# Order of the last steps of a weight fold, and the unread products ahead of it, in a fused attention and feed-forward kernel

## The chip, the cores and the metric

The kernel runs on one core of a Trainium2 chip. The metric is the device time of one execution in microseconds (us); lower is better. A core has TensorE (PE, matrix products; PEld is its loading of weights), VectorE (DVE), ScalarE (ACT), GpSimd (POOL) and SyncE (SP), which here issues nearly all DMA transfers. The engines run side by side, each in its own program order, and wait for each other by semaphores.

## The reference

```python
kv = einsum('bhsd,bhse->bhde', k, v)           # 8 batches, 8 heads, 576 x 64
out = einsum('bhsd,bhde->bhse', q, kv)
rms = sqrt(mean(out * out, axis=-1) + 1e-06)
x = (out / rms * g_norm), heads side by side   # 4608 x 512
a, b = x @ w1, x @ w2                          # 512 x 1024 each
h = (a * b) @ w3                               # 1024 x 1024
return h @ w_out                               # 1024 x 512
```

The weights come as 64-bit floats and are used as 32-bit floats.

## The kernel before, in words

`w3 @ w_out` doesn't depend on the tokens, so the kernel first folds the two into one matrix of 1024 x 512 (`w3o_sb`). That is the fold, the first 81 us. Then it goes over nine groups of 512 tokens: per group, attention, the gates (`x @ w1`, `x @ w2` and their product) and the projection by the folded matrix, the last two with a Winograd scheme that saves products by sums. The attention of the first batch is worked out between the fold's products.

**Conversion of weights.** A 64-bit weight tile (`raw`, four buffers, loaded at L207) is turned into 32-bit floats by two ScalarE passes (L165 for the low words, L167 for the high words) and four VectorE passes (L169, L173, L176, L181), with a scaling by g (L135) for w1 and w2. `begin_next` issues ScalarE's two, `end_next` the others and the next load; a conversion is a generator, so single steps can be issued apart.

**The fold.** `w3` is used in two halves of its columns, each in eight chunks of 128 rows. For each chunk TensorE transposes the piece of `w3` by four transposes (`turn_w3`, L701), ScalarE copies the result out of PSUM (L703) and `fold_chunk` runs four products of 512 columns (L717; in the first chunk eight of 256). A 32-bit product is two records in the trace. In the second half, chunks 3, 5 and 7 are transposed by a DMA instead: the words are taken apart (L308), the DMA transposes (L310), and a ScalarE copy, here called the join, puts the words together (L320, `ab<-chunks`). For chunk 7, "the eighth", the join was placed in iteration c = 5.

**Unread products.** `keep_warm(n, small)` (L282 to L287) issues n products of the identity with itself at 128 x 128, and `small` ones at 16 x 16. Nobody reads them. They stand at the start, before and after the first `turn_w3`, and once more (two) after the first chunk's fold.

**Attention of the first batch in the fold.** In iterations c = 1 and c = 4 `begin_q` transposes q and `begin_kv` works out kv; in c = 2 and c = 5 `product` computes the attention product (L425) and its norm: ScalarE squares two banks (L392), VectorE sums each (L393), ScalarE takes the root (L397), VectorE inverts it (L399) and multiplies (L402, two halves `xn`). The norm is a generator with a pause after the sums and one after the root. The first product's `xn` is taken apart by ScalarE (L306), transposed by two DMAs, and put together by VectorE (`x_by_dma`, L320, `xT<-xn`, "x's copies"). The second product's `xn` is transposed by TensorE at c = 7 (`turn`, L461) and copied by ScalarE (L463). Three fold products come after it, and then the gates of the first group (L748).

**What sets the order.** In this part the order on TensorE, VectorE, ScalarE, GpSimd and SyncE is that of the program (a manual schedule), so moving a call in the loop over c moves its instructions in the queues of its engines. Iteration c = 5 is the one that matters here: ahead of the fold's products it issues x's copies and then, for the weight tile whose conversion is under way, the three passes L169, L173 and L176 (one `next` on the conversion).

Of the kernel before, what the change touches and what calls it, by code (L numbers as in the profile page):

```python
# [22 lines left out]
def kernel(  # L23
# [60 lines left out]
    def bank(pool, tag):  # L84
        return pool.tile([P, 512], FP32, name=tag, tag=tag)
# [6 lines left out]
    def load_q(b, r):  # L92
        t = loaded["q", b, r] = inp.tile([P, 2, J * D], FP32, name="q_sb")
        nc.sync.dma_start(
            out=t, in_=q[b, 2 * r:2 * r + 2, 0:G, :].rearrange("h (p j) d -> p h (j d)", j=J)
        )

    def load_four(names, b, g):

        for name in names:  # L100
            t = loaded[name, b, g] = inp.tile([P, 2, JS * D], FP32, name=f"{name}_sb", bufs=1)
            src = dict(k=k, v=v)[name][b, 4 * g:4 * g + 4]
            src = src.rearrange("(r e) (p j) d -> (e p) r (j d)", e=2, j=JS)
            nc.sync.dma_start(out=t, in_=src)
# [95 lines left out]
    def load_next():  # L200
        if len(raws) == len(todo):
            return
        what, i = todo[len(raws)]
        raw = raw_tile()

        def load(where, src):
            nc.sync.dma_start(out=raw[:, where].rearrange("p (c m) -> p c m", c=src.shape[1]), in_=src)  # L207

        if what == "w":
            for n, w in enumerate((w1, w2)):  # L210
                src = w[:, i * P:(i + 1) * P].rearrange("(c p) f -> p c f", p=P)
                load(slice(n * 512, (n + 1) * 512), src)
        elif what == "b":
            for h in range(2):
                src = w3[DF // 2:DF, (2 * i + h) * P:(2 * i + h + 1) * P]
                load(slice(h * 512, (h + 1) * 512), src.rearrange("(m p) f -> p m f", p=P))
        else:
            src = w3[0:DF // 2, i * P:(i + 1) * P].rearrange("(m p) f -> p m f", p=P)
            cols = w_out[i * P:(i + 1) * P, :].rearrange("p (c f) -> p c f", c=1)

            n = 1 if i else 2
            for h in range(n):
                load(slice(h * 512 // n, (h + 1) * 512 // n), src[:, h * NH // n:(h + 1) * NH // n, :])
            for h in range(n):
                f = slice(h * DM // n, (h + 1) * DM // n)
                load(slice(512 + f.start, 512 + f.stop), cols[:, :, f])
        raws.append(raw)
# [21 lines left out]
    def begin_next(between=None, at=1):  # L249

        if len(begun) < len(todo):
            begun.append(conversions(len(begun)))
            for n, (c, _) in enumerate((c, i) for c in begun[-1] for i in range(2)):
                if between is not None and n == at:
                    between()
                next(c)

    def end_next(load=True):
        for c in begun[len(converted)]:
            all_of(c)  # L260
        converted.append(len(converted))
        if load:
            load_next()

    def all_of(steps):
        for _ in steps:
            pass
# [14 lines left out]
    def keep_warm(n, small=0):  # L282

        t = bank(ps_mm, "mm")
        for i in range(n + small):
            w = P if i < n else 16
            nc.tensor.matmul(t[0:w, 0:w], lhsT=ident[:, 0:w], rhs=ident[:, 0:w], start=True, stop=True)  # L287
# [409 lines left out]
    def turn_w3(half, c):  # L697
        t_ps = bank(ps_at, "at").rearrange("p (m f) -> p m f", m=NH)
        for m in range(NH):
            src = chunks[:, c, 0, m * P:(m + 1) * P]  # L700
            nc.tensor.transpose(t_ps[:, m, :], src, ident)  # L701

        nc.scalar.copy(place_w3(half, c), t_ps)  # L703
# [711 lines left out]
    with tc.manual_schedule(  # L1415
        engines={mybir.EngineType.DVE, mybir.EngineType.Activation, mybir.EngineType.SP}
    ):
        for _ in range(RAW):
            load_next()
        nc.scalar.activation(const.tile([P, 1], FP32, name="warm"), eps_col, AF.Sqrt)  # L1420
        g_row = const.tile([1, P], FP32, name="g_row")
        for e in range(2):
            nc.scalar.dma_start(
                out=g_row[:, e * D:(e + 1) * D], in_=g_norm.rearrange("(o d) -> o d", o=1)
            )


        keep_warm(14, 11)
        begin_next()
        end_next()  # L1430
        turn_w3(0, 0)
        keep_warm(6)
        begin_next()

        g_ps = bank(ps_at, "at")[:, 0:1]
        nc.tensor.transpose(g_ps, g_row, ident[0:1, 0:1])
        nc.scalar.copy(g_col, g_ps)
        for c in range(KF):

            if c > 2:  # L1440
                begin_next()
            end_next()
            if c == 4:
                load_four("k", 0, 0)
                load_q(0, 0)
            elif c == 5:
                load_four("v", 0, 0)
                load_q(0, 1)
                load_q_left(0)
            if c == 0:  # L1450
                for n in range(2):
                    fold_chunk(0, c, range(NH), slice(n * N, (n + 1) * N))
                begin_next(lambda: turn_w3(0, 1))
                keep_warm(2)
                continue
            fold_chunk(0, c, range(NH - 1))
            if c < 3:
                begin_next(lambda: turn_w3(0, c + 1), 2)
            else:
                turn_w3(*((0, c + 1) if c + 1 < KF else (1, 0)))  # L1460
            fold_chunk(0, c, [NH - 1])


        first = batch(0)
        first.start()
        BEGIN, PRODUCT = {1: 0, 4: 1}, {2: 0, 5: 1}
        norms = {}
        FIRST = len(converted) + KF - 1
        turns, SPLIT = {}, {0: 3, 2: 5, 4: 7}
        for c in range(KF):  # L1470
            if c in BEGIN:
                first.begin_q(2 * BEGIN[c], 2 * BEGIN[c] + 1)
                if c == max(BEGIN):
                    x_first = first.x_by_dma(0, nc.vector.tensor_copy, split=nc.scalar.copy)
                    next(x_first)
                    next(x_first)
                    all_of(turns[c + 1])
            if c - 1 in norms:
                all_of(norms[c - 1])
            if c < KF - 2:  # L1480
                if c < max(BEGIN):
                    begin_next()
                if c == max(BEGIN) + 1:
                    all_of(x_first)
                    for steps_of_w in begun[len(converted)]:
                        next(steps_of_w)
                else:
                    end_next(False)
                if c in SPLIT:
                    t = turns[SPLIT[c]] = w3_by_dma(SPLIT[c])  # L1490
                    next(t)
                    next(t)
                if len(raws) < FIRST:
                    load_next()
                if c == 2:
                    for steps_of_w in begun[len(converted)]:
                        next(steps_of_w)
                elif c == max(BEGIN):
                    run(sum_w(0))
            elif c == KF - 2:  # L1500
                end_next(False)
            fold_chunk(1, c, [0])
            if c in BEGIN:
                first.begin_kv(BEGIN[c])
                if c == max(BEGIN):
                    load_q_left(1)
            if c + 1 == KF:
                for r in range(2):
                    first.turn(2 + r)
                run(combine_x(0))  # L1510
                end_next(False)
                for _ in range(3):
                    load_next()
            fold_chunk(1, c, range(1, NH - 1))
            if c == 2:
                all_of(turns[c + 1])
            elif c + 1 < KF and c + 1 not in turns:
                turn_w3(1, c + 1)
                if c + 2 in turns and c > max(BEGIN):
                    all_of(turns[c + 2])  # L1520
            if c in (max(BEGIN), KF - 2):
                begin_next()
            fold_chunk(1, c, [NH - 1])
            if c in PRODUCT:
                norms[c] = first.product(PRODUCT[c])
                next(norms[c])
                next(norms[c])
    fold_cm.__exit__(None, None, None)
    late_pool = ctx.enter_context(tc.tile_pool(name="late", bufs=1, reuse_waits="tile"))
# [179 lines left out]
```

## Time and profile before

| | us |
|---|---|
| median of three runs (lowest, highest) | 741.62 (741.22, 742.58) |
| the profiled execution's own time | 742.19 |
| its span, first to last instruction | 740.4 |
| TensorE busy | 735.3 |
| VectorE busy | 628.1 |
| ScalarE busy | 378.7 |
| DMA, HBM traffic over the span | 204 GB/s |

The profile is one execution, and its times are counted from the start of the span. A line of the timeline has the start, the duration, the engine, the line of the program, the operation, the tile written and the tile read, and how often; in brackets stands the idle time ahead of it and what ended it. Lines that follow each other on one engine may be merged. In the lines of a groups or waits view the numbers are the total, how often, and the longest. Matmuls overlap in the array and their ends are modelled, so a busy TensorE isn't TensorE at its peak.

### The profile page before, as it was taken

The page shows a single profiled execution, that of the slowest core. Times are in us where ns is not written, and L with a number is a line of the kernel's source. Part 1 is how long each engine was busy: PE and PEld are TensorE (multiplying, and loading weights), DVE is VectorE, ACT ScalarE, POOL GpSimd, SP SyncE. Part 2 cuts the span into 40 slices and gives each one's busy share as a digit, 9 for nine tenths or more (in the row PEclk, how much of TensorE's full clock was granted, in tenths as well). Part 3 has the DMA queues.
Part 4 walks back from the last instruction along what each step waited for, and adds up shares of the span by engine and source line. Part 5 has one row for each costly group of instructions (what it writes and reads, how often), then busy time and mean ns, then how long its engine had stood idle before and what let it go on. Part 6 is the DMA issues. An engine that isn't in the chain of part 4 may idle for free.

```text
span 740.4 us, 16916 instructions
## 1 busy us (share of the span) xinstructions
PE 735.3 (99%) x6863; PEld 660.5 (89%) x6863; DVE 628.1 (85%) x1259; ACT 378.7 (51%) x660; POOL 22.2 (3%) x29
## 2 busy tenths in 40 slices
PE   9999999999999999999999999999999999999998
PEld 7455788888899999999999999999999999999998
DVE  6987898968869689968996899689969987997797
ACT  6787777415552675257526752576177313212321
POOL 0000000132000000000000001000001000000000
PEclk9999999999999999999999999999999999999999
DMA  9999934599989698859986998598847762465354
GB/s 314 331 342 240 288 108 134 131 347 297 318 262 320 174 278 261 268 162 291 260 263 174 281 258 265 179 284 237 275 101 221 222 212 87 175 216 165 130 198 143
DMA packets 138769, 170.44 MB, mean 230 GB/s; under 512 B 81220, under 2 KB 114116, under 8 KB 138692
## 3 DMA queue, kind: packets, MB, share of 16 engines
q1 hardware_dynamic: 136240, 155.02, 70.6%
q10 hardware_dynamic: 2452, 14.35, 5.7%
q8 instruction: 54, 0.88, 0.5%
q14 instruction: 23, 0.19, 0.1%
HBM read 130.55 MB, written 20.71 MB: 204 GB/s over the span
## 4 chain that ended last, share of the span: by engine, by line
PE 97%; ACT 1%; DVE 1%; DMA 1%; issue 0%; POOL 0%; SPq 0%; DVEq 0%; POOLq 0%
PE mm L748 38%; PE mm L1298 23%; PE mm L1040 21%; PE mm L717 6%; PE at L347 2%; PE at L748 2%; PE mm L287 1%; PE mm L425 1%; PE at L425 1%; PE at L701 1%; DMA xn<-xT 1%; PE at L1341 0%; PE at L444 0%; DVE inv L393 0%; ACT xT L306 0%
## 5 line engine op out<-in xcount | busy, mean ns | idle before, releaser
L1089 ACT COPY slots<-mm 128x512 f32<-128x512 f32 x88 | 51.6, 586 | 127.0 <-PE mm L1298 83.7
L748 PE MATMUL mm<-xT,w_sb 128*128 128x256 f32 x448 | 102.9, 379 | 0.0
L748 PEld LDWEIGHTS mm<-xT,w_sb 128*128 128x128 f32 x448 | 84.4, 190 | 11.5 <-issue 0.5
L748 PE MATMUL mm<-xc,ws 128*128 128x256 f32 x336 | 76.1, 379 | 0.0
L748 PEld LDWEIGHTS mm<-xc,ws 128*128 128x128 f32 x336 | 63.9, 190 | 8.7
L766 ACT COPY slots<-mm 128x512 f32<-128x512 f32 x59 | 34.5, 585 | 70.6 <-PE mm L748 65.6
L717 PE MATMUL mm<-chunks,ab 128*128 128x512 f32 (+1 forms) x136 | 59.9, 578 | 0.3 <-ACT ab L703 0.2
L1093 DVE TENSOR_TENSOR slots<-mm,slots 128x512 f32<-128x512 f32 x66 | 45.1, 683 | 17.2 <-PE mm L1040 17.1
L1090 ACT COPY slots<-mm 128x384 f32<-128x384 f32 x88 | 42.3, 481 | 26.3 <-PE mm L1298 23.8
L1040 PE MATMUL mm<-ws,w3o_sb 128*128 128x128 f32 x350 | 53.9, 275 | 0.0
L1298 PE MATMUL mm<-w3o_sb,ab 128*128 128x128 f32 x368 | 48.9, 276 | 0.0
L393 DVE TENSOR_REDUCE inv<-sq 128x8 f32<-128x512 f32 (+1 forms) x40 | 24.6, 630 | 27.2 <-ACT sq L392 27.2
L1040 PEld LDWEIGHTS mm<-ws,w3o_sb 128*128 128x128 f32 x350 | 46.4, 192 | 0.0
L1298 PEld LDWEIGHTS mm<-w3o_sb,ab 128*128 128x128 f32 x368 | 45.4, 192 | 0.6
L717 PEld LDWEIGHTS mm<-chunks,ab 128*128 128x128 f32 x136 | 23.6, 190 | 22.5 <-issue 15.5
L1298 PE MATMUL mm<-w3o_sb,raw 128*128 128x128 f32 x340 | 43.5, 275 | 0.0
L1298 PEld LDWEIGHTS mm<-w3o_sb,raw 128*128 128x128 f32 x340 | 40.7, 192 | 0.0
L748 PE MATMUL mm<-xc,w_sb 128*128 128x256 f32 x160 | 38.5, 384 | 0.0
L1094 DVE TENSOR_TENSOR slots<-mm,slots 128x384 f32<-128x384 f32 x66 | 36.3, 551 | 2.2 <-PE mm L1298 1.6
L748 PE MATMUL mm<-xT,ws 128*128 128x256 f32 x160 | 38.1, 381 | 0.0
L748 PEld LDWEIGHTS mm<-xT,ws 128*128 128x128 f32 x160 | 30.1, 190 | 4.3 <-ACT slots L766 0.2
L748 PEld LDWEIGHTS mm<-xc,w_sb 128*128 128x128 f32 x160 | 29.8, 190 | 4.2
(246 smaller groups left out, 1650.0 us busy)
## 6 DMA issues: line engine op xcount, KB each, us to landing
w3o_sb<-w_l SPq DMA_DIRECT2D x21, 896.0 KB, 5.6
w3o_sb<-w3o_l SPq DMA_DIRECT2D x18, 896.0 KB, 6.0
raw<-in_moe_w_dram SPq DMA_DIRECT2D x31, 512.0 KB, 7.5
raw<-w3o_l SPq DMA_DIRECT2D x15, 896.0 KB, 4.7
w3o_sb<-w3o_l ACTq DMA_DIRECT2D x14, 896.0 KB, 4.6
k_sb<-in_k_dram SPq DMA_DIRECT2D x16, 576.0 KB, 5.7
v_sb<-in_v_dram SPq DMA_DIRECT2D x16, 576.0 KB, 6.3
q_sb<-in_q_dram SPq DMA_DIRECT2D x32, 256.0 KB, 4.8
```

The costliest lines, as they stand in the source:

```text
L347: nc.tensor.matmul(ps[r * D:(r + 1) * D, :], lhsT=k_sb[rows, r, cols], rhs=v_sb[rows, r, cols], start=(j == 0), stop=(j == JS - 1),)
L393: adds["norm"] = nc.vector.tensor_reduce(out=inv[:, i], in_=sq.rearrange("p (h d) -> p h d", d=D), axis=AX.X, op=ALU.add)
L425: nc.tensor.matmul(o_ps[l][tokens, n * D:(n + 1) * D], lhsT=qT[r][rows, e, i, tokens], rhs=kv_b[rows, m // 2 ^ l, e, h, :], start=True, st ...
L717: nc.tensor.matmul(sums_ps[half][m][:, cols], lhsT=w3T[half, c][:, m, :], rhs=chunks[:, c, 1, cols], start=(c == 0 and cols.start == 0), s ...
L748: nc.tensor.matmul(ps[:, u, :], lhsT=lhsT(a_name, u, c), rhs=rhs(b_name, c),  start=(u == 0 and c == 0 and new), stop=(c == chunks - 1), s ...
L766: copies.setdefault(name, []).append(nc.scalar.copy(t, ps))
L1040: nc.tensor.matmul(ps[place // 4][:, place % 4, :], lhsT=x, rhs=y, start=new and place // 4 not in seen, stop=True, skip_group_check=True,)
L1089: nc.scalar.copy(z[:, 0:4], ps[0])
L1090: return nc.scalar.copy(z[:, 4:7], ps[1][:, 0:3])
L1093: nc.vector.tensor_add(z[:, 0:4], ps[0], z[:, 0:4])
L1094: nc.vector.tensor_add(z[:, 4:7], ps[1][:, 0:3], z[:, 4:7])
L1298: nc.tensor.matmul(ps[place // 4][:, place % 4, :], lhsT=x[:, c, :], rhs=y[:, c, :], start=new and place // 4 not in seen, stop=(c == 1), ...
```

## The change

Three things are done, and the numbers of instructions of each kind stay as they are but for the unread products.

1. At the start, ahead of the first transposes, 11 large unread products instead of 14 large and 11 small. Behind these transposes, 1 large and 21 small instead of 6 large.
2. In iteration c = 5 the three VectorE passes over a weight tile (L169, L173, L176) are issued ahead of x's copies (L320) and not behind them.
3. In the same iteration the join of the eighth chunk (ScalarE, L320 `ab<-chunks`) is issued behind the two squares of the second norm and ahead of its root, not ahead of the squares.

The orders of SyncE and GpSimd, and so of the DMA transfers, are the same in both kernels.

```diff
-        keep_warm(14, 11)
+        keep_warm(11)
         begin_next()
         end_next()
         turn_w3(0, 0)
-        keep_warm(6)
+        keep_warm(1, 21)
         begin_next()
...
                 if c == max(BEGIN) + 1:
-                    all_of(x_first)
                     for steps_of_w in begun[len(converted)]:
                         next(steps_of_w)
+                    all_of(x_first)
                 else:
                     end_next(False)
...
             elif c + 1 < KF and c + 1 not in turns:
                 turn_w3(1, c + 1)
-                if c + 2 in turns and c > max(BEGIN):
-                    all_of(turns[c + 2])
             if c in (max(BEGIN), KF - 2):
                 begin_next()
             fold_chunk(1, c, [NH - 1])
             if c in PRODUCT:
                 norms[c] = first.product(PRODUCT[c])
                 next(norms[c])
+                if c > max(BEGIN):
+                    all_of(turns[c + 2])
                 next(norms[c])
```

## The prediction

> **What bounds the kernel now.** I read the page first: busy shares, then the chain that ended last.
>
> ```profile
> span 740.4 us, 16916 instructions
> PE 735.3 (99%) x6863; PEld 660.5 (89%) x6863; DVE 628.1 (85%) x1259; ACT 378.7 (51%) x660; POOL 22.2 (3%) x29
> PE 97%; ACT 1%; DVE 1%; DMA 1%; issue 0%; POOL 0%; SPq 0%; DVEq 0%; POOLq 0%
> ```
>
> TensorE bounds the kernel: it has work in 735.3 of 740.4 us. Next, what it waited for in the whole run:
>
> ```profile
> PE mm L287 <- POOL ident masks.py:199: 1.4, 1, 1.4
> PE at L461 <- DVE xn L402: 0.5, 2, 0.3
> PE mm L717 <- ACT ab L703: 0.2, 1, 0.2
> ```
>
> From about 79 us to the last transposes nothing is listed: TensorE is never seen to wait there. So the change can win only ahead of 79 us, in two places: the unread products (L287), which count as busy but give nothing, and the two waits at L461. Whatever is won there comes through, if no other engine then falls behind. The timeline of the start:
>
> ```profile
> 6.50 0.43 DVE L181 CUSTOM_DVE_ANT_0 chunks<-chunks,ab 128x512 uint16<-128x512 uint16 x1
> 7.38 0.42 ACT L167 ACTIVATE chunks<-raw 128x256 f32<-128x256 f32 x1
> 7.89 0.66 PE L701 MATMUL at<-ident,chunks 128*128 128x128 f32 x4
> 8.38 1.50 PE L287 MATMUL mm<-ident 128*128 128x128 f32 x12
> 8.58 0.58 ACT L703 COPY ab<-at 128x512 f32<-128x512 f32 x1 [0.77 <-PE at L701]
> 9.81 0.22 PE L1436 MATMUL at<-ident,g_row 1*128 1x1 f32 x1
> ```
>
> The data of the first transposes are there at 6.93 (6.50 + 0.43), but TensorE, still in unread products, starts them at 7.89. The copy of their result is done at 9.16; the fold's first product starts at 9.96, behind six more unread products. So the unread products, not the data, set the start. The timeline of the end of the fold:
>
> ```profile
> 71.43 1.30 DVE L320 COPY xT<-xn 128x1024 uint16<-128x1024 uint16 x2 [2.47 <-ACT ab L703]
> 72.33 1.17 ACT L320 COPY ab<-chunks 128x1024 uint16<-128x1024 uint16 x1 [1.00 <-DMA chunks<-ab]
> 72.65 0.75 DVE L169 TENSOR_SCALAR ab<-raw 128x1024 uint16<-128x1024 uint16 x1
> 73.28 0.68 DVE L173 TENSOR_SCALAR w_sb<-w_sb 128x1024 f32<-128x1024 f32 x1
> 73.40 1.07 ACT L392 ACTIVATE sq<-at 128x512 f32<-128x512 f32 x2
> 74.00 0.69 DVE L176 TENSOR_SCALAR w_sb<-w_sb 128x1024 uint32<-128x1024 uint32 x1
> 74.61 1.27 DVE L393 TENSOR_REDUCE inv<-sq 128x8 f32<-128x512 f32 x2
> 75.91 0.31 ACT L397 ACTIVATE inv<-inv,eps_col 128x16 f32<-128x16 f32 x1 [1.44 <-DVE inv L393]
> 76.61 1.29 DVE L402 TENSOR_TENSOR xn<-at,inv 128x512 f32<-128x512 f32 x2
> 77.35 0.33 PE L461 MATMUL at<-ident,xn 128*128 128x128 f32 x1 [0.20 <-DVE xn L402]
> 77.95 0.98 PE L461 MATMUL at<-ident,xn 128*128 128x128 f32 x7 [0.27 <-DVE xn L402]
> ```
>
> VectorE sits idle for 2.47 us (68.97 to 71.43), then its three weight passes stand ahead of the reduces; ScalarE puts the join ahead of the squares, though the attention product was done at 72.66. TensorE pays at L461.
>
> **Part 1: the unread products.** A 128-wide unread product is two records. In the profile 22 records fill the first 4.85 us (windows view, 1.35 to 6.20), 0.213 us each; later (8.38) they come every 0.111. So TensorE ran at half rate for the first 5.4 us. The page's clock row (tenths of 40 slices) is too coarse to show it.
>
> Removed at first: 3 large (6 records) and 11 small. The 11 that stay end at 6.20. Two transposes follow at once (their quarter was ready at 5.44), the third waits until 6.98, the fourth's result is there by 7.36. ScalarE is in L167 until 7.80, so the copy L703 runs 7.80 to 8.38 instead of 8.58 to 9.16. Meanwhile TensorE does one large product (0.22) and 21 small ones: 42 records. In the profile 22 small records took 0.61 us (windows view, 7.24 to 7.85), nearly 0.025 us apart, so 42 take 1.05. From 7.20: 0.22, 0.1 for the change of shape, 1.05, then 0.1 and 0.15 around the transpose of g (L1436, as in the trace): the fold's first product at 8.82, not 9.96: **−1.14 us**. It is the small products, not the copy (8.38), that set it.
>
> Does the rest follow? The fold of chunk 0 ends at 12.38; chunk 1's first half is ready at 11.95 even as before. Its second half was ready at 13.81 and will be wanted at 13.65; but VectorE had idled 0.46 behind ScalarE's L165 at 9.06, which can now start when its load lands (2.80 + 5.8 = 8.6), so 13.4. If that cover fails, 0.16 is lost. For chunk 2 VectorE had waited 1.16 at 15.34 for a pass queued behind L703: that goes with TensorE. From there VectorE needs 3.75 us a chunk and TensorE 3.96. Loads: chunk 6 lands at 24.5 and is read at 26.7, 2.2 us of cover.
>
> What no row shows is the pace of small products at half rate. Below: 0.025, as seen. Above: twice that, as the large ones do (0.213 to 0.111), 1.05 us more, and the part is worth 0.1. I take 0.025, since in the profile the clock had doubled at 6.8, before they start.
>
> A rule speaks against the change here. The trace doubled its rate 5.4 us after the first product. The Trainium skill ("TensorE: Matmul & The Clock Gate", Part 1: The HAM clock gate) says that the clock is released after one busy window of about 3.4 us, free-running, so the moment differs between runs; its Part 4 says that transposes don't count as busy in the same way. By that rule, windows that end after 6.2 are less busy than before, and some executions would be released a window (3.4 us) later: the estimate from the page is about 1 us back in these runs. No row here shows it.
>
> **Part 2: weight passes first.** Nothing is added; L169, L173, L176 (0.75, 0.68, 0.69) go into the idle 2.47 us. L169's input ends at 68.73, L173's at 69.76 (ScalarE, 68.63 + 1.13), so they run 68.97 to 71.2, and the x copies, whose transposes land at 71.3, keep their 71.43. Cost nothing, cover 0.2 us; if gone, the reduces still have 0.6. No DMA is in the moved steps, and SP's and POOL's orders are unchanged. One load that waited 0.5 us for L176 may start earlier: 0 to a trifle.
>
> **Part 3: the join behind the squares.** Squares at 72.72 (0.06 behind the product, as in the first norm, 57.66 to 57.72) instead of 73.40, to 73.79. Reduces at 73.36 and 73.96 (copies done 72.73) to 74.63. The join, whose data land at 72.3, now runs 73.70 to 74.87; root at about 74.8 (ScalarE's starts lie 1.07 apart behind such a copy), not 75.91: 1.1 us earlier. The root is thus held by the join for some 0.1 us, no more. Normalized halves at 76.2 and 76.8, not 77.3 and 77.9. TensorE's last product starts at 76.55, so it wants them at 76.98 and 77.1: both waits go. Without them eight transposes take 0.87 (0.109 each) and the next product starts at 77.86 instead of 78.77: **−0.91 us**; the view's 0.47 understates it, since the ends of products are modelled and count as busy beyond the next possible start. Queued behind the later join are the root, the next weight passes (L165, L167), L723 and the x copies L463: all still earlier than before by about 0.8. TensorE wants the join's result for the eighth chunk at 75.7 (weight load); it is there at 74.9. What is late next: the second normalized half, 0.3 us of cover.
>
> **Sum:** 742.19 (profiled: span 740.4 and 1.79 around it) − 1.14 − 0.91 = **740.1**. The median of the runs shown is 741.62, so −0.2% of it. The runs spread from 741.22 to 742.58; a release of the clock earlier or later than 6.8 moves the old start of the fold (1 us earlier release, six to nine records from half to full rate, 0.5 us), while the new one, which waits for data at 6.98, hardly moves. I therefore sum from the profile and not from the median.
>
> **Rivals.** *Half the gain:* one of the two is lost to something not seen, say the first 14 us catch up with the conversions (13.81), or another engine is late further on, since TensorE arrives 2 us earlier everywhere and covers there can't be read from a view without waits. 742.19 − 1.14 = 741.05 or 742.19 − 0.91 = 741.28. For: VectorE is 92% busy from 10 to 41 us (28.48 of 31.0). Against: its waits there are for ScalarE, which waits for TensorE.
>
> *Slower: the clock is released late.* With only transposes, gaps and 16-wide products between 6.2 and 8.8, the work there may not count. If TensorE then needs as much full work again as at the start (5.4 us) from the fold's first product on, half of it, 2.7, is lost, and up to 1.05 more in the small products: 743.0 to 744.0 (740.14 + 2.7 to + 3.75). It decides where half rate lasts beyond about 4 us into the fold. For: the trace holds no case of so little work before a release. Against: large products still fill 1.35 to 6.20, and 22 small records and four transposes (7.24 to 8.38) did not take the rate back.
>
> **Chances.** Forecast 0.62, from 739.7 (fold bound by the copy, 0.4 earlier) to 740.8; half the gain 0.23, 740.8 to 741.5; late clock 0.15. "Within 0.2%" (about what a measurement of this kernel can tell from no change) begins at 740.14, on the forecast itself: of its 0.62 I put 0.47 beyond, since the four times shown average 741.9, over the median, and 0.15 within. Faster 0.47, same 0.15 + 0.23 = 0.38, slower 0.15. The range is 739.7 to 741.5, which leaves the late clock out.
>
> **What would show it.** The fold's first L717 at 8.8; no wait at L461 and its eight transposes in one row; L169 at 69 minus 1.1, ahead of L320; squares, join, root in this order, root about 1.1 us after the squares end. Wrong: unread or fold products 0.43 us apart in the 256-wide records after 9 us (late clock), a wait of L717 at 13.6 for L181, or new waits of TensorE after 79 us.

## The result, and the profile after

| | before | after |
|---|---|---|
| median, us (16 runs each) | 742.38 | 740.40 |
| lowest and highest | 741.22, 743.29 | 740.02, 740.94 |
| profiled execution, own time | 742.19 | 740.67 |
| its span | 740.4 | 738.8 |

The change makes the kernel 1.98 us faster by the medians; the ratio is 0.9975, with a 95% interval of 0.9968 to 0.9983. The median of before over 16 runs lies 0.76 above that of the three runs shown ahead of the prediction. Between the two profiled executions the difference is 1.52, less than between the medians. The runs after lie closer together: within 0.92 us, before within 2.07.

The page after still has TensorE as the bound. But the chain now has a transfer in it, 2% `raw` and SyncE, where before it had 1% `xn`:

```profile
span 738.8 us, 16924 instructions
PE 733.8 (99%) x6867; PEld 659.5 (89%) x6867; DVE 629.1 (85%) x1259; ACT 378.9 (51%) x660; POOL 22.2 (3%) x29
PE 94%; DMA 2%; ACT 2%; DVE 1%; SPq 1%; issue 0%; ACTq 0%
```

What TensorE waited for in the whole run after:

```profile
PE mm L287 <- POOL ident masks.py:199: 1.4, 1, 1.4
PE mm L717 <- DVE chunks L181: 0.5, 1, 0.5
PE mm L748 <- ACT inner_sums L766: 0.3, 1, 0.3
```

The waits at L461 are gone. Two others are there in their place: one in the fold's second chunk, at L181 where there had been 0.2 at L703, and one in the gates, at L748, where before had none. The timeline of the start, after:

```profile
1.35 5.06 PE L287 MATMUL mm<-ident 128*128 128x128 f32 x22 [1.35 <-POOL ident masks.py:199]
6.21 1.02 PE L701 MATMUL at<-ident,chunks 128*128 128x128 f32 x4
6.30 0.42 DVE L181 CUSTOM_DVE_ANT_0 chunks<-chunks,ab 128x512 uint16<-128x512 uint16 x1
8.10 0.57 ACT L703 COPY ab<-at 128x512 f32<-128x512 f32 x1
8.53 0.22 PE L1436 MATMUL at<-ident,g_row 1*128 1x1 f32 x1
8.72 3.72 PE L717 MATMUL mm<-chunks,ab 128*128 128x256 f32 x16
```

The transposes now stand around the end of the second quarter's conversion (6.72), and the fold starts at 8.72 instead of 9.96, 0.05 behind the end of the copy (8.67). The timeline of the end of the fold, after:

```profile
67.71 0.75 DVE L169 TENSOR_SCALAR ab<-raw 128x1024 uint16<-128x1024 uint16 x1
69.37 0.69 DVE L176 TENSOR_SCALAR w_sb<-w_sb 128x1024 uint32<-128x1024 uint32 x1
70.31 1.30 DVE L320 COPY xT<-xn 128x1024 uint16<-128x1024 uint16 x2 [0.25 <-DMA xn<-xT]
71.58 1.09 ACT L392 ACTIVATE sq<-at 128x512 f32<-128x512 f32 x2 [1.44 <-PE at L425]
72.21 1.28 DVE L393 TENSOR_REDUCE inv<-sq 128x8 f32<-128x512 f32 x2 [0.60 <-ACT sq L392]
72.55 1.16 ACT L320 COPY ab<-chunks 128x1024 uint16<-128x1024 uint16 x1
73.60 0.32 ACT L397 ACTIVATE inv<-inv,eps_col 128x16 f32<-128x16 f32 x1
74.31 1.29 DVE L402 TENSOR_TENSOR xn<-at,inv 128x512 f32<-128x512 f32 x2
75.80 1.04 PE L461 MATMUL at<-ident,xn 128*128 128x128 f32 x8
```

The passes fill VectorE's idle time, the sums start with the first square's end, the join stands between squares and root, and the eight transposes of L461 are one row. The new wait stands four microseconds behind the fold's last product, at the third product of the gates:

```profile
79.25 1.89 PE L748 MATMUL mm<-xT,w_sb 128*128 128x256 f32 x8
80.97 1.89 PE L748 MATMUL mm<-xc,ws 128*128 128x256 f32 x8
83.12 1.13 PE L748 MATMUL mm<-xc,ws 128*128 128x256 f32 x4 [0.26 <-ACT inner_sums L766]
```

The chain of waits after, followed back from there, says what it hangs on (start, duration, what):

```profile
71.60 0.62 SPq L207
...
72.27 8.51 DMA raw<-in_moe_w_dram
...
80.94 0.25 ACT ab L165
...
82.01 0.57 ACT w3o_sb L723
82.58 0.49 ACT inner_sums L766
83.08 0.04 issue
83.12 2.00 PE mm L748 x8
```

A load of `raw` lands at 80.78; ScalarE's L165 waits for it, and queued behind L165 are L723 and L766, whose bank the third product wants. The timeline after names another for this wait, VectorE's L169, which ends at 80.79:

```profile
80.04 0.75 DVE L169 TENSOR_SCALAR ab<-raw 128x1024 uint16<-128x1024 uint16 x1
80.94 1.17 ACT L165 ACTIVATE ab<-raw 128x1024 f32<-128x1024 uint32 x1 [1.46 <-DVE ab L169]
```

The same two before:

```profile
81.48 1.20 ACT L165 ACTIVATE ab<-raw 128x1024 f32<-128x1024 uint32 x1
82.33 0.75 DVE L169 TENSOR_SCALAR ab<-raw 128x1024 uint16<-128x1024 uint16 x1
```

There L165 started without a wait and 0.85 ahead of this L169, so it doesn't need it, and the load is what is left.

How far TensorE is ahead of before, product by product: 1.24 at the fold's first product, 0.95 at chunk 1 (13.84 for 14.79), 1.17 from chunk 2 (17.79 for 18.96), 1.19 ahead of L461, 2.10 behind it (76.67 for 78.77) and at the first product of the gates (79.25 for 81.35), 1.57 from the second record of the third on (83.44 for 85.02), 1.54 at the end.

### The profile page after: what moved, and what is told of

Its sections match the earlier page's. It is cut to its first block, busy times and chain, and to the rows that moved or that the text cites. A ratio compares the mean times of both kernels' runs of the same rounds, so it can differ in the third digit from the quotient of the medians.

```text
span 738.8 us, 16924 instructions
## 1 busy us (share of the span) xinstructions
PE 733.8 (99%) x6867; PEld 659.5 (89%) x6867; DVE 629.1 (85%) x1259; ACT 378.9 (51%) x660; POOL 22.2 (3%) x29
## 4 chain that ended last, share of the span: by engine, by line
PE 94%; DMA 2%; ACT 2%; DVE 1%; SPq 1%; issue 0%; ACTq 0%
PE mm L748 37%; PE mm L1298 23%; PE mm L1040 21%; PE mm L717 5%; PE at L347 2%; DMA raw<-in_moe_w_dram 2%; PE at L748 2%; PE mm L425 1%; PE at L425 1%; PE at L701 1%; PE at L1341 0%; ACT ab L165 0%; SPq L207 0%; PE at L444 0%; ACT xT L306 0%
## 5 line engine op out<-in xcount | busy, mean ns | idle before, releaser
L748 PE MATMUL mm<-xT,w_sb 128*128 128x256 f32 x448 | 102.9, 380 | 0.0
L748 PEld LDWEIGHTS mm<-xT,w_sb 128*128 128x128 f32 x448 | 84.6, 191 | 11.3 <-issue 0.5
L748 PE MATMUL mm<-xc,ws 128*128 128x256 f32 x336 | 76.4, 380 | 0.3 <-ACT inner_sums L766 0.3
L748 PEld LDWEIGHTS mm<-xc,ws 128*128 128x128 f32 x336 | 63.9, 190 | 9.1 <-ACT inner_sums L766 0.7
L766 ACT COPY slots<-mm 128x512 f32<-128x512 f32 x59 | 34.6, 586 | 70.0 <-PE mm L748 65.0
L717 PE MATMUL mm<-chunks,ab 128*128 128x512 f32 (+1 forms) x136 | 59.7, 578 | 0.5 <-DVE chunks L181 0.5
L717 PEld LDWEIGHTS mm<-chunks,ab 128*128 128x128 f32 x136 | 23.6, 190 | 22.6 <-issue 15.5
L748 PE MATMUL mm<-xc,w_sb 128*128 128x256 f32 x160 | 38.5, 384 | 0.0
L748 PE MATMUL mm<-xT,ws 128*128 128x256 f32 x160 | 38.2, 382 | 0.0
L748 PEld LDWEIGHTS mm<-xT,ws 128*128 128x128 f32 x160 | 30.1, 190 | 4.2 <-ACT slots L766 0.2
L748 PEld LDWEIGHTS mm<-xc,w_sb 128*128 128x128 f32 x160 | 29.9, 190 | 4.2
```

Source lines behind the costliest of these rows:

```text
L717: nc.tensor.matmul(sums_ps[half][m][:, cols], lhsT=w3T[half, c][:, m, :], rhs=chunks[:, c, 1, cols], start=(c == 0 and cols.start == 0), s ...
L748: nc.tensor.matmul(ps[:, u, :], lhsT=lhsT(a_name, u, c), rhs=rhs(b_name, c),  start=(u == 0 and c == 0 and new), stop=(c == chunks - 1), s ...
L766: copies.setdefault(name, []).append(nc.scalar.copy(t, ps))
```

## The experiments

No experiment keeps the DMA transposes. Each replaces them by plain DMA copies of the same bytes, so the data stay untransposed and the outputs are not the reference's. The base is therefore the kernel before with the same replacement, and whether one part alone does the same with the transposes in place wasn't tried. The runs were taken on several chips, on which the medians of the kernel before lay between 741.97 and 742.61; so a difference between the times of two experiments is exact to some 0.6 only, unless both ran on one chip, as the base and the changed kernel with the same replacement did. The ratios are to the kernel before on the same chip, and a comparison of starts within the traces doesn't depend on this.

**A first base, pieces of 128 bytes** (two copies in place of each transpose).

```diff
-        nc.sync.dma_start_transpose(
-            out=turned.bitcast(U16).rearrange("p (a t) -> p a t", t=P), in_=apart.bitcast(U16)
-        )
+        pieces = [t.bitcast(U16).rearrange("p (c h t) -> p h c t", h=2, t=64) for t in (turned, apart)]
+        for h in range(2):
+            nc.sync.dma_start(out=pieces[0][:, h], in_=pieces[1][:, h])
```

> The kernel before, in which every DMA transpose is replaced by two plain DMA copies of the same 256 KB in pieces of 128 bytes: the data stay untransposed, so the output is not the reference's. It is the base for the experiments. Theory: until 44 us nothing differs; at the end of the fold x's copies come when two copies of 256 KB land (4.6 us for the transposes), so if these land in 4 to 5 us the two waits at L461 (0.2 and 0.3) stand as before and the time is within 1 us of the kernel before. If they land much earlier, VectorE's passes run earlier and the waits at L461 shrink.

> The changed kernel with the same replacement. Theory: against the base with the replacement, the same steps as in the changed kernel: first L717 at 8.7, a wait of about 0.5 us for L181 at 13.8, no wait at L461. The wait of L748 at 83 us should be smaller or gone if the loads of raw are issued earlier than 71.6 (two plain copies may hold SyncE for less time than a transpose), and should stand if they are issued at 71.6. Total 1.5 to 2.1 us below the base. Rival (the gain hangs on the transposes themselves): under 1 us.

Measured: 746.44 (742.58 to 749.25) and 744.75 (741.08 to 746.30). The expectation for the base failed: TensorE waits 2.5 us at L461 there, and 1.6 and 0.9 in the projections. The changed kernel missed its own as well: it waits 0.6 at L461, where none was expected, and 1.1 at L748. The base is too disturbed to measure a change of 2 us, and the pair is not used further, except for the start of the fold (9.67 and 8.95).

**The base used, pieces of 256 bytes in the fold, one plain copy afterwards** (in these files each line behind L312 counts one more: L462 is L461, L749 is L748).

```diff
+        n = 1 if in_first_group else 2
+        pieces = [t.bitcast(U16).rearrange("p (c h t) -> p h c t", h=n, t=128) for t in (turned, apart)]
+        for h in range(n):
+            nc.sync.dma_start(out=pieces[0][:, h], in_=pieces[1][:, h])
```

> The kernel before, with the DMA transposes of the fold replaced by two plain copies each (256 KB together, pieces of 256 bytes) and the later ones by one plain copy, so that the data stay untransposed and the output is not the reference's. A quieter base than the one with pieces of 128 bytes, which held SyncE for 1.5 us per copy and gave 742.6 to 749.3. Theory: x's copies on VectorE start at 70 to 72 us, the two waits at L461 stand with 0.3 to 0.6 us together, no wait of TensorE behind 79 us, time within 1.5 us of the kernel before.

> The changed kernel with the same replacement as the base just named. Theory: first L717 at 8.7, a wait of about 0.5 for L181 at 13.8, no wait at L461; total 1.5 to 2.1 us below the base, less what a wait of L748 near 83 us takes if the load of raw read there is issued no earlier than 71 us. Rival (the gain hangs on the transposes themselves): under 1 us.

Measured: 741.83 (740.49 to 742.54) and 740.56 (740.43 to 741.57), a difference of 1.27; the ratios are 0.9989 (0.9979 to 0.9998) and 0.9979 (0.9969 to 0.9989). By the two profiles TensorE is 0.80 ahead at the fold's first product and 1.30 behind L461, to the end. So both steps stand without the transposes; the sum is less than expected, since in the profiled execution of the changed kernel the data came late (second quarter done at 7.10), and since x's copies come 0.5 us earlier in this base, which leaves only the second of the two waits. The wait of 0.5 for L181 at 13.8 didn't come either: chunk 1 waits 0.23 for its copy, as in the base. The wait in the base:

```profile
76.88 0.31 PE L462 MATMUL at<-ident,xn 128*128 128x128 f32 x1
77.46 0.98 PE L462 MATMUL at<-ident,xn 128*128 128x128 f32 x7 [0.27 <-DVE xn L403]
```

No wait at L749 came after the change here. The load that L165 waited for landed before it mattered.

**Only the unread products** (`keep_warm(11)`, `keep_warm(1, 21)` in the base).

> The base with plain copies (741.83 median); of the change only the unread products. Theory (two separate gains): the fold's first L717 (one line further down in this file) 0.8 to 1.2 us earlier than 9.84; the wait at L461 (here L462) stays at 0.27 (0.42 between starts of products), and TensorE's lead of 0.8 to 1.2 is the same behind it as ahead of it. 740.6 to 741.0. Rival (the early start is lost at the end of the fold, whose norm hangs on the transfers of x): the wait at L462 grows by as much as the start gains, 741.6 or more.

Measured: 741.12 (740.66 to 742.65), ratio 0.9988 (0.9978 to 0.9998). The runs alone can't tell it from the base. The profile can: the fold's first product at 8.65 for 9.85, TensorE 1.20 ahead up to L462 and 0.92 from there on to the end, the wait at L462 unchanged at 0.27. So the start's lead is carried through but for 0.28, which the x transposes take because the first normalized half is 0.9 earlier and not 1.2. The rival is ruled out in the profile but for these 0.28, and the size of the gain in the time stays unresolved.

**Only passes and join.**

> The base with plain copies; passes and join moved, unread products as before. Theory: no wait at L462, 0.42 us gained there and kept, no wait of L748 near 83. 741.3 to 741.6. Rival (the moved join or the later loads take it back): 741.8 or more, with a wait of L717 for the join at 76 or of L748 at 83.

Measured: 741.03 (740.32 to 741.66), ratio 0.9984 (0.9975 to 0.9993). In the profile TensorE enters the end of the fold 0.25 ahead (its fold started at 9.59) and leaves it 0.72 ahead, so 0.47 is gained there, as expected (0.42). The time lies 0.27 below the expected range; the early start of the profiled execution is about that much, but it is one execution. The transposes are one row:

```profile
76.63 1.04 PE L462 MATMUL at<-ident,xn 128*128 128x128 f32 x8
```

**Passes alone, join alone.** The two moved blocks of the diff, one without the other, one run each.

> The base with plain copies; only the three passes moved. In this base x's copies start at 70.92 and the squares at 73.48, behind the join. Theory (the sums wait for the later of L176 and the squares): with L176 out of the way they still wait for the squares, which end at 74.03 and 74.56, so root at 75.4 as in the base and the wait at L462 stays within 0.1. Rival (the passes were the cause): root 0.6 earlier, no wait at L462.

> The base with plain copies; only the join moved. Theory: squares 1.0 earlier (72.5), but the sums wait for L176 until 74.1, so root at 75.4 and the wait at L462 stays within 0.1. Rival (the join was the cause): root 0.6 or more earlier, no wait at L462.

The timelines, first with the passes alone:

```profile
71.73 1.16 ACT L321 COPY ab<-chunks 128x1024 uint16<-128x1024 uint16 x1 [1.16 <-DMA chunks<-ab]
72.80 1.08 ACT L393 ACTIVATE sq<-at 128x512 f32<-128x512 f32 x2
73.42 1.28 DVE L394 TENSOR_REDUCE inv<-sq 128x8 f32<-128x512 f32 x2 [1.63 <-ACT sq L393]
76.78 0.98 PE L462 MATMUL at<-ident,xn 128*128 128x128 f32 x7 [0.27 <-DVE xn L403]
```

Then with the join alone:

```profile
72.78 1.08 ACT L393 ACTIVATE sq<-at 128x512 f32<-128x512 f32 x2 [1.44 <-PE at L426]
73.57 0.69 DVE L176 TENSOR_SCALAR w_sb<-w_sb 128x1024 uint32<-128x1024 uint32 x1
74.18 1.27 DVE L394 TENSOR_REDUCE inv<-sq 128x8 f32<-128x512 f32 x2
77.53 0.99 PE L462 MATMUL at<-ident,xn 128*128 128x128 f32 x7 [0.26 <-DVE xn L403]
```

With the passes out of the way VectorE sits idle for 1.63 us until the squares, which stand behind the join. With the join out of the way the squares are early, and the sums wait for L176. The wait at L462 stays at 0.27 and 0.26. In this base each part alone gains nothing at L462: TensorE's lead is 0.65 ahead of L462 and behind it in the one, and 0.13 behind the base at both ends in the other. The two moves gain together. (Times: 741.16 and 741.86; the first had its fold start at 9.21.)

**Four large unread products ahead, in place of 11** (`keep_warm(4)` in the changed kernel with plain copies): the price of a late clock.

> The changed kernel with plain copies, with 4 large unread products ahead of the first transposes in place of 11: TensorE idles from about 3.2 us to the first transposes and between them. Theory of the late clock: less work ahead of 7 us releases the full rate later, between 9 and 14 us; products of the fold's first chunk 0.43 apart until then, 0.5 to 2.7 us lost against the changed kernel with plain copies (740.56). Rival (the data set the start, and how much TensorE works ahead of them doesn't matter): first L717 at 8.6 to 9.1, full rate there, within 0.3 us of 740.56.

Measured: 741.65 (741.15 to 742.12), 1.09 over the 740.56 with 11, and 1.42 in the profiled executions. The timeline of its start:

```profile
1.35 2.08 PE L287 MATMUL mm<-ident 128*128 128x128 f32 x8 [1.35 <-POOL ident masks.py:199]
5.59 0.69 PE L702 MATMUL at<-ident,chunks 128*128 128x128 f32 x2 [2.16 <-DVE chunks L181]
7.27 1.87 PE L287 MATMUL mm<-ident 128*128 128x128 f32 x44
9.26 4.95 PE L718 MATMUL mm<-chunks,ab 128*128 128x256 f32 x16
```

The fold's 16 records take 4.95 us and not 3.72: until 11.8 they come every 0.427, from then on every 0.216. So the slower rival of the prediction is a real mechanism, with a price of 1 to 1.5 us when the work ahead is cut to four products; with 11 it set in in none of the seven executions profiled. The copy (L704) was done at 8.17, so here the unread products alone held the fold back. The 42 small records came 0.027 apart at half rate, against 0.025 at full rate: the unknown pace that the prediction bounded by 0.025 and 0.05.

**Five small unread products behind the transposes, in place of 21.**

> The changed kernel with plain copies, with 5 small unread products behind the first transposes in place of 21 (0.4 us less of them). Theory (with 21 the start is already set by the data: the copy of the transposes ends within 0.3 us of the first L717, and chunk 1 waits for its conversion at L181 anyway): first L717 0 to 0.4 earlier, first product of chunk 1 where it was, 13.8, with a longer wait; the time the same within 0.2 us. Rival (the small products set the time, as the prediction had it): 0.4 us faster.

Measured: 740.24 (739.57 to 741.46), ratio 0.9973 (0.9963 to 0.9982) against 0.9979 (0.9969 to 0.9989) with 21. The medians, 0.32 apart, lie between the two theories, and the intervals overlap. The unread products became 0.80 shorter (0.73 for 1.53), not 0.4 as the expectation says. The theory's premise doesn't hold in the profiled execution with 21: there the copy ended at 8.59 and the fold began at 9.04, 0.45 later, so the small products set the start and up to 0.4 was to be won. In the profiled execution with five, the slowest of its runs, the loads came late: the fold's first product waits 0.9 for the copy (9.22), and chunk 1 waits 0.5 for L181 (14.32). What the shorter filling is worth in a usual run stays open.

**Loads of `raw` later** (tiny loads on SyncE ahead of the three that follow 71.6, in the changed kernel with plain copies): three, then six.

```diff
                 end_next(False)
+                unread = [const.tile([P, 8], FP32, name=f"unread{i}") for i in range(3)]
+                for i in range(6):
+                    nc.sync.dma_start(out=unread[i % 3], in_=q[i, 0, 0:P, 0:8])
                 for _ in range(3):
                     load_next()
```

> The changed kernel with plain copies, and three tiny loads (128 x 32 bytes, into tiles that nobody reads) on SyncE ahead of the three loads of raw behind 71.6 us, so that these come about 1.2 us later. Theory (in the changed kernel the load of raw that L165 reads at 81 became late, held back L723 and L766 behind it on ScalarE, and so the bank that L748 wants at 83): L165 waits 1.2 to 1.8 us for the load, where it waited 0.5, and TensorE now waits 0.3 to 0.7 us at L748 (one line further down here) near 83 us, where it did not wait. Rival (the wait near 83 in the changed kernel comes from the order of ScalarE, and the load has room): no wait of TensorE there.

> As the run with three tiny loads, but six, two into each tile, so that the loads of raw come at least 2.5 us later than in the changed kernel with plain copies (71.6). Theory (L165 behind this load holds back L723 and L766 on ScalarE and so the bank that the third product of L748 wants): L165 waits 2 to 4 us, and TensorE waits 1.0 to 3.0 us ahead of the third product of L748 (3.4 us behind the first), time 0.7 to 2.5 us over 740.56. Rival (the load has room, the wait in the changed kernel came from the order of ScalarE): no wait there, 740.5.

Measured with three: 740.57 (740.21 to 741.90). L165 waited 1.14, just under the range; TensorE had been held for 0.9 by another load (`v_sb`) in the profiled execution, and the gap ahead of the third product grew by only 0.1, and by 0.1 behind it. The place is the expected one, but the size is too small to decide. With six the loads of `raw` left at 78.49 in place of 71.62, far later than the 2.5 us asked for: 743.18 (742.50 to 746.27), 2.62 over 740.56. The waits of TensorE and the timeline of ScalarE there:

```profile
PE mm L749 <- ACT inner_sums L767: 2.4, 1, 2.4
83.83 1.15 ACT L165 ACTIVATE ab<-raw 128x1024 f32<-128x1024 uint32 x1 [3.51 <-DMA raw<-in_moe_w_dram]
84.87 0.58 ACT L767 COPY inner_sums<-mm 128x512 f32<-128x512 f32 x1
```

TensorE stands until 85.50 ahead of the third product, and its delay of 2.6 goes through to the end unchanged. A late load of `raw` does hold the gates at this point. What wasn't tried is the counterpart, an earlier load in the changed kernel with its transposes.

## Why the prediction was right

The forecast was 740.1 (739.7 to 741.5); measured were 740.40 by the median and 740.67 by the profiled execution. The two terms of the sum are right in mechanism and in size; what the sum lacked is 0.5 us that was lost behind the fold.

- *What bounds:* right. TensorE's lead at 85 us (1.57) is the gain at the end (1.54).
- *The start, −1.14:* measured −1.24. Eleven large products ended at 6.2, two transposes followed at once, and the third waited for the second quarter. The small products were said to set the start and not the copy. In the execution measured the two end together: the copy ended at 8.67, 0.3 later than forecast, and the fold started at 8.72. In four of the other five executions with 21 small products the copy was done 0.29 to 0.45 ahead of the fold, as the prediction had it.
- *Chunk 1:* the prediction named a loss of 0.16 if VectorE's cover failed. The cover failed, since the load that L165 reads, taken to land at 8.6, let it start at 8.93 only. A wait of 0.52 for L181 came, a loss of 0.29 against the lead of 1.24; from chunk 2 on the lead was 1.17 again, since before had waited there as well.
- *The passes:* right, at no cost. L169 starts 0.2 earlier than "69 minus 1.1", and x's copies wait 0.25 for their transfer.
- *The join, −0.91:* measured −0.91 (1.19 to 2.10). Squares, join and root come in this order, and the join holds the root back by 0.1 (the sums end at 73.49, the root starts at 73.60), as said. Starts of products were the right measure, not the listed waits (0.47).
- *The sum:* −2.05 forecast at the end of the fold, −2.10 measured at the gates. Then 0.5 was given back, and this is what the sum lacked: the wait at L748. The prediction had it as a risk without a price ("covers there can't be read from a view without waits"). It could have been read. In before, L165 started at 81.48 while its load, issued as the second of a pair at 72.9, landed at 81.05: a cover of 0.4, against a TensorE that was to come 2 us earlier.
- *"SP's order is unchanged":* right, but its timing didn't follow TensorE. The DMA transpose that stands ahead of these loads held SyncE for 1.79 us before and for 2.47 after, so the loads left only 0.5 earlier, and the one that counts landed only 0.3 earlier. The queue before:

```profile
68.12 1.79 SPq L310 DMA_TRANSPOSE chunks<-ab  x1
72.10 7.45 SPq L207 DMA_DIRECT2D raw<-in_moe_w_dram  x6
```

The same queue after:

```profile
66.94 2.47 SPq L310 DMA_TRANSPOSE chunks<-ab  x1
71.60 7.64 SPq L207 DMA_DIRECT2D raw<-in_moe_w_dram  x6
```

- *The late clock:* didn't come with 11 large products (full rate from 4.41 to 7.04 in the seven executions profiled), and did with four, at a lower price than the rival named (2.7 or more was said, 1.1 to 1.45 measured). The rule of the Trainium skill that spoke against the change ("TensorE: Matmul & The Clock Gate", Part 1: The HAM clock gate) holds in that the moment differs from run to run. The estimate of 1 us back that the prediction worked out from it wasn't seen. The point of the page's Part 4, that transposes count less, is not decided by these runs.
- *The page's clock row:* it isn't too coarse, as the prediction has it. The windows view gives a granted clock of 1.00 for 1.35 to 6.20 too, where the records come at half the pace; the clock record of the trace starts only with the step to the full rate. The pace of the records is what shows it.
- *The signs of being wrong:* two of the three that were named came, a wait of L717 for L181 at 13.8 and a new wait of TensorE after 79 us. They cost 0.07 (1.24 to 1.17) and 0.5, and the forecast held in spite of them.
- *Faster by over 0.2%:* the measured −0.25% falls beyond this line, though the interval (−0.17% to −0.32%) reaches back over it. There is luck in it: the median of before was higher over 16 runs than over three, and between the medians the difference (1.98) is nearer to the sum (2.05) than between the two executions (1.52), for which it was worked out.

That the old start hung on the clock and the new one on the data is seen across the profiled executions (us; full rate from the trace's clock record, the second quarter by the end of its L181, the copy by the end of L703):

| unread products ahead | kernel | full rate from | second quarter | copy done | first fold product |
|---|---|---|---|---|---|
| 14 large, 11 small | passes alone | 4.68 | 7.12 | 9.12 | 9.21 |
| | passes and join | 5.99 | 7.24 | 9.04 | 9.59 |
| | first base | 6.15 | 7.25 | 9.26 | 9.67 |
| | base | 6.53 | 7.39 | 9.05 | 9.85 |
| | before | 6.77 | 6.92 | 9.16 | 9.96 |
| | join alone | 6.80 | 6.68 | 9.18 | 9.98 |
| 11 large | unread products alone | 5.56 | 6.71 | 8.28 | 8.65 |
| | after | 6.61 | 6.73 | 8.67 | 8.72 |
| | changed, first base | 7.04 | 7.01 | 8.50 | 8.95 |
| | changed, plain copies | 7.00 | 7.10 | 8.59 | 9.04 |
| | three tiny loads | 6.19 | 7.27 | 8.93 | 9.21 |
| | six tiny loads | 5.79 | 6.70 | 9.01 | 9.06 |

In the upper rows the start follows the clock, about 0.47 per microsecond (0.5 was said), and not the data; only in the first row the clock came so early that the copy set the start. In the lower ones it lies 1.94 behind the data in four rows, whenever the clock came: that is the time of the last two transposes and of the unread products behind them. So the data now say when this work begins, but the unread products are still what the fold waits for there, by 0.29 to 0.45 us. In the other two, after and six tiny loads, the copy sets the start.

The narrower spread of the times after isn't explained by this. The starts in the upper rows differ by 0.77 us and the runs before by 2.07; before has one of the latest starts of its group and a time under its median; and with the unread products alone the ten runs spread over 1.99, as in the base (2.05). So it stays open what narrowed the spread, and why the medians differ by more than the two profiled executions.

## What to carry to other kernels

Work that only fills time should end before the data that it bridges come, or it becomes the limit; here the cut is safe as long as it doesn't delay the full clock rate, as cutting it to four products did. When two things stand ahead of a step on two engines, moving one alone may gain nothing, so ask what is late next before you judge it. When the bound engine is to come 2 us earlier, list the loads that are read within the next stage, with the time they land and the time they are used: a view of waits shows none of those that are still covered by half a microsecond.

## What the runs showed of the hardware

- The moment at which TensorE went from half to full rate lay between 4.41 and 7.04 us in thirteen executions with the same first product at 1.35 and at least 11 large products, and at 11.8 in one with four.
- 16 x 16 products cost nearly the same at half rate (0.027 us a record) as at full rate (0.025); 128-wide ones cost about double (0.213 and 0.111).
- One DMA transpose of 256 KB held SyncE's queue between 1.2 and 4.2 us, while the loads behind it waited, and the one for the eighth chunk took 0.7 us more after than before.
- Copies of 128 KB in pieces of 128 bytes held the queue for 0.6 to 4.2 us each in the fold, and with two of them in place of each of the 69 transposes the kernel took 4.5 us more than before on the same chip; in pieces of 256 bytes they held it for 0.6 to 1.5, and with the later transfers in one copy each the kernel was 0.1% faster than with the transposes.
